# Left operands loaded in place, weight sums on two engines, and a rearranged opening in a Strassen-like gated MLP

## The chip, the cores and the metric

The kernel runs on one core of a Trainium2 chip. The metric is the device time of one execution in microseconds; lower is better. All arithmetic is in 32-bit floats. TensorE (PE) reads them as fp32r, which drops low bits, so each operand is split into a high part and a low part and a product is made of three: high x high, high x low, low x high.

## The reference, cut to what matters

```python
x = A_x                                   # 2048 x 576
g = sigmoid((x * gate_w).sum(-1, keepdims=True))
a = linear_attention(x, wqkv) @ wo        # 32 heads
h = gelu(x @ w_gate) * (x @ w_up)         # 576 -> 4608
b = h @ w_down                            # 4608 -> 576
return g * a + (1 - g) * b
```

## The kernel before, in words

There are three stages. The first, up to about 271 us, makes the attention part and stores g * a to DRAM. It isn't touched.

**Gate and up chains.** `x @ w_gate` and `x @ w_up` are done by Strassen's scheme with seven block products (`PRODUCTS`; `product`, whose matmuls are at L854) instead of eight. One chain is one matrix (GATE or UP), one block n of 256 of the 4608 columns, and one half p of the rows; `CHAINS` lists all 72. A product is 7 matmuls of 128x128 by 128x512. Chain c runs in two frames: in frame c its products 1, 6 and 2, in frame c+1 its products 7, 5, 3 and 4, interleaved with the next chain's by the order `FRAME = 1, 7, 5, 3, 6, 2, 4`. So a frame has seven slots, and `(frame, slot)` is an address. Everything that isn't a product is put at such an address with `put(frame, i, do)`; what stands at an address is issued behind that slot's product, and each engine executes in the order of issue.

A chain takes four PSUM banks from a pool of eight: "a" and "b" at slot 0 (the seed of "b" is a ScalarE copy of "a"), "d" at slot 2 and "c" at slot 4. Of its four result blocks, number 0 comes from "a", 3 and 1 from "d" and "b" after additions on VectorE (DVE, `d_sum` is the ScalarE copy of the fifth product, L967; the additions are L969, L972, L979, L982), 2 from "c". A gate chain runs gelu over them (L929) into SBUF; an up chain multiplies onto that (`up`, L932). The blocks live in `e` (p = 0) and `f` (p = 1).

The weights W[GATE] and W[UP] have seven blocks each: three raw ones and four sums. `w_fetch` (L858) loads the four raw blocks into `wraw` and lets GpSimd (POOL) add the sums into `tsum` (`weight_sums`, L373); for (1, UP) the sums come from DRAM (`ws_d`, L860). `w_split` makes the high part on ScalarE (ACT, L868) and the low part on POOL (L869, L870). For the second half of the rows, X[1] is built in the first frames: blocks A11, A12, A22 by DMA (`X_AT`, L1266), the four sums in six pieces (`S_AT`, `s_make`: ACT L1224, then DVE or POOL L1225; `s_load` L1219), each piece through one of two halves of `f`.

**What down needs.** `h @ w_down` is done with 26 products of blocks of h (`DOWN`, one line each: left operand, weight sum, seed, which accumulators it goes to, which weight sums are made for it). The left operands (sums and differences of h blocks named "a7b6" and the like) are made on DVE during the chains by `extras(c)` (`add` L992, `sub` L995), a table by frame and slot relative to chain c, and stored to DRAM (L1004); `get` loads parts back (L1010). For the last chain (LAST = 71) the entries after a certain address are kept in a list `late` and done during the first down units.

**Down units.** A product is cut in three (c = 0, 1, 2), so there are 78 units, `UNITS[u] = (m, c)`. A unit is 36 matmuls 128x128 by 128x288 (L1340). Unit u's left operand (768 KB) is loaded to one of up to four raw buffers (`h_load`, L1196) and split by `h_make`: high part on ACT (L1203, L1206), low part on DVE (L1204, L1207), into `hb[u % 4]`. Its weight is split by `make`: high on ACT (L1173), low on POOL (L1174). Weight sums (`sums`, L1168) go to DVE if the product's left operand has one part and to POOL if it has two; the tiles `vt` come by `fetch` (L1157). The main loop runs `unit(u, 0)`, then `h_make(u + 3)`, `w_make(u + 3)`, `w_sums(u + 4)`, `later()`, `unit(u, 1)`, `later()`. When a product is complete (c = 2), DVE adds its banks onto the accumulators that read it (L1350); a product with "c" in its line goes on in the same banks, so its matmuls wait for those adds. The three first units' operands and weights are prepared by addresses in the last frames.

Of the kernel before, what the change touches and what calls it, by code (L numbers as in the profile page):

```python
# [11 lines left out]
OP = mybir.AluOpType  # L12
# [102 lines left out]
def tile_gated_mix(ctx, tc, xt, xs, xn, wk, wv, wq, wo, wgu, wdn, cst, out):  # L115
# [805 lines left out]

    def chain(c):
# [3 lines left out]
        d_sum = mid["p1"]  # L926
# [4 lines left out]
        def up(i, src):  # L931
            nc.vector.tensor_tensor(es[i], src, es[i], OP.mult)  # L932
# [31 lines left out]
        def s5():  # L964
            d = bank()
            product(p, 5, w, d, True)
            nc.scalar.activation(d_sum, d, AF.Copy)  # L967
            if m == GATE:
                nc.vector.tensor_tensor(es[3], ps["c"], d_sum, OP.add)  # L969
                gelu(3)  # L970
            else:
                nc.vector.tensor_tensor(d, ps["c"], d_sum, OP.add)  # L972
                up(3, d)
# [38 lines left out]
    def extras(c):  # L1012
# [7 lines left out]

        def do(op, o, a, b, name=None):
            def run():
                op(o, a, b)
                if name:
                    keep_h(g, name, o)
            return run
# [35 lines left out]
        return {(-1, 5): [get("7", r0), get("x", r1), get("y", r2)],  # L1062
                (0, 3): [get("6", e[0])],
                (0, 4): [get("5", e[3])],
                (0, 5): [do(add, e[1], e[1], f[0])],
                (0, 6): [do(add, e[1], e[1], r0, "a7b7")],
                (1, 0): [do(sub, e[0], e[0], f[0], "a6b6"), do(add, r0, r0, f[0], "a7b6")],
                (1, 1): [do(sub, r2, f[0], r2, "ayb6")],
                (1, 2): [do(add, s0, s0, f[3])],
                (1, 3): [do(add, s0, s0, e[3], "a5b5"), get("4", r0), get("9", r2)],  # L1070
                (1, 4): [do(add, e[3], e[3], f[3], "a5b4"), do(add, s1, f[0], f[1], "bx")],
                (1, 5): [do(add, r1, r1, s1, "axbx"), do(add, f[1], f[1], f[3], "bz")],
                (1, 6): [do(sub, r0, r0, f[3], "a4b4"), hold("b8", f[2])],
                (2, 0): [do(sub, e[2], f[2], e[2]), do(add, e[2], e[2], r2, "a9b9")],
                (2, 1): [do(add, s2, s1, f[3], "by"), get("8", r1)],
                (2, 3): [do(add, s1, r2, f[2], "a9b8")],
                (2, 4): [do(sub, r2, s2, r2, "a9by")],
                (2, 5): [do(sub, r1, f[2], r1, "a8b8")]}

# [18 lines left out]
    wraw, tsum = (stage[:, c:c + 1536].rearrange("p (i k c) -> p i k c", i=4, k=3) for c in (0, 1536))  # L1098
    es += [e123[:, i] for i in range(3)]
# [25 lines left out]
    class Weights:  # L1125


        def __init__(self):
            self.tasks, self.last, self.at, self.free = [], {}, {}, list(range(18))
# [30 lines left out]
        def sums(self, j):  # L1160
            m, c = UNITS[j]
            for name, x, op, y in DOWN[m].made:
# [4 lines left out]
                eng = nc.vector if len(DOWN[m].parts) == 1 else nc.gpsimd  # L1167
# [10 lines left out]
    AHEAD = 4  # L1178
# [10 lines left out]
    loads, raw_of = deque(range(len(UNITS))), {}  # L1189
# [8 lines left out]
    def h_make(j):  # L1198
        if j < len(UNITS):
            h, at = hb[j % 4], raw_of.pop(j)  # L1200
            raw = raw_at[at]
# [6 lines left out]
            raw_free.append(at)  # L1208
# [32 lines left out]

    ALL = (0, 3), (3, 7)
# [4 lines left out]
    for c, m, more in ((2, UP, (2, GATE)), (5, GATE, (2, UP))):  # L1247
        split_at(c, 0, m, (0, 2))
        split_at(c, 1, m, (4, 5))
        split_at(c, 3, m, (5, 6), (3, 4))  # L1250
        split_at(c, 4, m, (2, 3))
        split_at(c + 1, 0, m, (6, 7))
        fetch_at(c + 1, 0, *more)
    split_at(7, 0, UP, *ALL)
    fetch_at(7, 5, 3, GATE)
# [30 lines left out]
    for frame, i, do in ((LAST - 4, 6, lambda: w_sums(0, 2)), (LAST - 1, 1, lambda: h_load()), (LAST - 1, 1, lambda: w_make(0)),  # L1286
                         (LAST - 1, 2, lambda: w_sums(1, 2)), (LAST - 1, 4, lambda: h_make(0)),
                         (LAST - 1, 5, lambda: w_make(1)), (LAST, 0, lambda: w_sums(2, 1)), (LAST, 2, lambda: h_make(1)),
                         (LAST, 3, lambda: w_make(2)), (LAST + 1, 0, lambda: raw_free.extend((1, 2))),
                         (LAST + 1, 0, lambda: h_make(2)), (LAST + 1, 3, lambda: w_sums(3, 0))):  # L1290
        put(frame, i, do)
# [62 lines left out]
    def later():  # L1354
        if late:
            for do in late.pop(0):
                do()
            if not late:
                raw_free.append(3)

    weight.fetch(7)
    h_load()
# [85 lines left out]
```

## Time and profile before

| | |
|---|---|
| median of 3 runs | 1537.33 us (1535.36 to 1538.04) |
| profiled execution | 1533.54 us, of which the span of the program's instructions is 1531.8 |
| PE matmul busy | 1460.6 us, 95% of the span |
| VectorE, ScalarE, GpSimd busy | 959.5, 640.4, 784.0 us |
| mean granted PE clock | 0.983 of full speed |
| DMA | 282.32 MB, 184 GB/s in the mean |

Matmuls are pipelined and their ends are modelled, so PE busy isn't PE at its peak. The chains begin at about 271 us, the down units at 1109.5 us. In a row of the timeline stand start, length, engine, line, operation, names (out <- in), shapes and, in brackets, how long the engine sat idle before it and what ended that. Names have their numbers left out, and pieces cut from one tile have the tile's name: `xo` is also the space for the down operands.

### The profile page before, as it was taken

The page shows a single profiled execution, that of the slowest core. Times are in us where ns is not written, and L with a number is a line of the kernel's source. Part 1 is how long each engine was busy: PE and PEld are TensorE (multiplying, and loading weights), DVE is VectorE, ACT ScalarE, POOL GpSimd, SP SyncE. Part 2 cuts the span into 40 slices and gives each one's busy share as a digit, 9 for nine tenths or more (in the row PEclk, how much of TensorE's full clock was granted, in tenths as well). Part 3 has the DMA queues.
Part 4 walks back from the last instruction along what each step waited for, and adds up shares of the span by engine and source line. Part 5 has one row for each costly group of instructions (what it writes and reads, how often), then busy time and mean ns, then how long its engine had stood idle before and what let it go on. Part 6 is the DMA issues. An engine that isn't in the chain of part 4 may idle for free. (4 is left out here: it accounts for less than half of the span.)

```text
span 1531.8 us, 21118 instructions
## 1 busy us (share of the span) xinstructions
PE 1460.6 (95%) x8096; PEld 1296.4 (85%) x8096; DVE 959.5 (63%) x1121; ACT 640.4 (42%) x863; POOL 784.0 (51%) x505
## 2 busy tenths in 40 slices
PE   9999999889999999999999999999689899989989
PEld 9998899778878878787887878788589889989979
DVE  7887896434384654647455374743778568759474
ACT  7555664434333334333333433333334354435342
POOL 2663451545455454455445545541136885685763
PEclk9999999999999999999999999999889999999999
DMA  7664567642453433536344353547989475665651
GB/s 245 173 191 151 181 212 245 213 170 73 152 206 124 166 136 114 175 124 211 128 142 162 107 200 124 190 147 239 314 317 370 146 245 177 224 233 193 215 184 55
DMA packets 122629, 282.32 MB, mean 184 GB/s; under 512 B 11864, under 2 KB 39064, under 8 KB 121248
## 3 DMA queue, kind: packets, MB, share of 16 engines
q1 hardware_dynamic: 119792, 273.71, 52.7%
q10 hardware_dynamic: 2736, 7.28, 1.3%
q8 instruction: 63, 1.03, 0.3%
q14 instruction: 38, 0.31, 0.1%
HBM read 182.40 MB, written 98.50 MB: 183 GB/s over the span
## 5 line engine op out<-in xcount | busy, mean ns | idle before, releaser
L854 PE MATMUL bank<-xo,wg 128*128 128x512 f32 x1764 | 419.8, 391 | 17.8 <-DVE e L969 9.9
L854 PE MATMUL bank<-xo,wu 128*128 128x512 f32 x1715 | 405.7, 390 | 4.6 <-DVE bank L972 2.9
L854 PEld LDWEIGHTS bank<-xo,wg 128*128 128x128 f32 x1764 | 331.1, 188 | 90.5 <-DVE e L969 12.8
L854 PEld LDWEIGHTS bank<-xo,wu 128*128 128x128 f32 x1715 | 323.2, 189 | 72.9 <-DVE bank L972 3.3
L1340 PE MATMUL bank<-xo 128*128 128x288 f32 x2124 | 294.7, 300 | 28.9 <-DVE acc L1350 27.0
L1340 PEld LDWEIGHTS bank<-xo 128*128 128x128 f32 x2124 | 289.6, 192 | 32.4 <-DVE acc L1350 16.8
L373 POOL TENSOR_TENSOR stage<-stage 128x384 f32<-128x384 f32 x132 | 138.6, 1071 | 178.7 <-DMA stage<-wgu 176.1
L939 ACT ACTIVATE bank<-bank 128x512 f32<-128x512 f32 x139 | 80.9, 582 | 242.1 <-PE bank L854 238.5
L1174 POOL TENSOR_TENSOR xo<-vt,xo 128x864 fp32r<-128x864 f32 x42 | 107.7, 2564 | 78.5 <-ACT xo L1173 76.1
L869 POOL TENSOR_TENSOR wg<-stage,wg 128x768 fp32r<-128x768 f32 (+3 forms) x41 | 73.8, 1800 | 136.5 <-ACT wg L868 131.9
L1174 POOL TENSOR_TENSOR xo<-stage,xo 128x864 fp32r<-128x864 f32 x26 | 68.5, 2635 | 103.2 <-ACT xo L1173 90.6
L869 POOL TENSOR_TENSOR wu<-stage,wu 128x768 fp32r<-128x768 f32 (+3 forms) x38 | 75.7, 1993 | 84.1 <-ACT wu L868 82.5
L972 DVE TENSOR_TENSOR bank<-bank,mid 128x512 f32<-128x512 f32 x36 | 25.1, 697 | 142.7 <-ACT mid L967 142.7
L1340 PE MATMUL bank<-xo,wu 128*128 128x288 f32 x684 | 96.1, 299 | 5.2 <-DVE acc L1350 5.2
L1340 PEld LDWEIGHTS bank<-xo,wu 128*128 128x128 f32 x684 | 93.6, 192 | 5.8 <-issue 3.6
L969 DVE TENSOR_TENSOR f<-bank,mid 128x512 f32<-128x512 f32 x18 | 12.4, 691 | 118.5 <-ACT mid L967 114.2
L967 ACT ACTIVATE mid<-bank 128x512 f32<-128x512 f32 x71 | 42.4, 597 | 96.8 <-PE bank L854 88.6
L1173 ACT ACTIVATE xo<-vt 128x864 fp32r<-128x864 f32 x42 | 38.7, 921 | 81.3 <-POOL vt L1168 53.6
L781 PEld LDWEIGHTS pair<-kw,p 128*128 128x128 f32 x448 | 60.8, 189 | 1.0
L781 PE MATMUL pair<-kw,p 128*128 128x288 f32 x448 | 61.4, 295 | 0.0
L531 PE MATMUL bank<-xo,qw 128*128 128x512 f32 (+1 forms) x231 | 55.7, 392 | 0.0
L932 DVE TENSOR_TENSOR f<-bank,f 128x512 f32<-128x512 f32 x72 | 49.6, 688 | 6.7 <-PE bank L854 5.4
(245 smaller groups left out, 2166.8 us busy)
## 6 DMA issues: line engine op xcount, KB each, us to landing
wg<-h_d SPq DMA_DIRECT2D x39, 768.0 KB, 5.1
stage<-wgu SPq DMA_DIRECT2D x34, 768.0 KB, 4.3
h_d<-sx SPq DMA_DIRECT2D x72, 256.0 KB, 3.5
xo<-h_d SPq DMA_DIRECT2D x22, 768.0 KB, 8.6
h_d<-mid SPq DMA_DIRECT2D x63, 256.0 KB, 4.3
h_d<-e SPq DMA_DIRECT2D x63, 256.0 KB, 3.5
e<-h_d SPq DMA_DIRECT2D x17, 768.0 KB, 4.5
vt<-wdn SPq DMA_DIRECT2D x25, 432.0 KB, 5.5
```

The lines of the kernel that those rows point to most:

```text
L373: nc.gpsimd.tensor_tensor(o, a, b, OP.subtract)
L531: nc.tensor.matmul(ps[:wa.shape[1]], wa, xa, start=(k == 0), stop=(k == len(ops) - 1), skip_group_check=g == 4)
L781: nc.tensor.matmul(y[:, i, :288], p[:, 5 * a + g], KW[g][:, wl, i * 288:(i + 1) * 288], start=(n == 0), stop=(n == 13))
L854: nc.tensor.matmul(ps, w_, x_, start=start and i == 0, stop=i == 6, skip_group_check=not start)
L869: nc.gpsimd.tensor_tensor(w[:, i, 3:5], src[:, :, 0:2], f32(w[:, i, 0:2]), OP.subtract)
L932: nc.vector.tensor_tensor(es[i], src, es[i], OP.mult)
L939: nc.scalar.activation(o, src, AF.Copy)
L967: nc.scalar.activation(d_sum, d, AF.Copy)
L972: nc.vector.tensor_tensor(d, ps["c"], d_sum, OP.add)
L1173: nc.scalar.activation(w[:, 0], src, AF.Copy)
L1174: nc.gpsimd.tensor_tensor(w[:, 1], src, f32(w[:, 0]), OP.subtract)
L1340: nc.tensor.matmul(y, h[:, hl, g, t * 128:(t + 1) * 128], w[:, wl, g * 288:(g + 1) * 288], start=first and c == 0 and n == 0, stop=c == NK ...
```

## The change

1. *First left operands in place.* Units 0, 1 and 2 have their left operand loaded straight into the place of its low part, `hb[u][:, 1]` (`h_direct`), at (LAST-2, 1), (LAST-1, 0) and (LAST, 0); `h_make` then splits it there. The raw buffers begin with unit 3. The splits of units 1 and 2 move from (LAST, 2) and (LAST+1, 0) to (LAST, 4) and (LAST+1, 6).
2. *Weight sums.* They go to POOL for c = 1, and for c = 2 if the product's number is odd, else to DVE. They run five units ahead instead of four. The first weight tiles are fetched at (LAST-4, 6); the sums of unit 3 are made at (LAST, 5), those of unit 4 ahead of the loop.
3. *Two up blocks stay in banks.* In the chains (p = 1, UP, n odd and over 1: eight of them) blocks 0 and 3 are multiplied in place in banks "a" and "d", and the additions of `extras` read them there. One of these additions moves from (2, 1) to (1, 6), one from (2, 0) to (2, 1), and two fetches move by a slot.
4. *Early splits.* The three raw blocks of (1, UP) are loaded at (0, 5) into a space of their own (`wmore`) and split from there; the splits of the first two frames, X pieces and blocks stand at other addresses; the sums of (2, GATE) get an address of their own; the splits of UP at frame 7 come in two parts.
5. *Leftovers.* Two more entries of the last chain go to `late`, which is now served once per unit, not twice. `vt` starts with 15 tiles and gets three more when `late` is empty. Accumulator loads move from units 1, 3, 6 to units 5, 10, 18.

```diff
-        d_sum = mid["p1"]
+        d_sum, in_bank = mid["p1"], m == UP and p == 1 and n > 1 and n % 2 == 1
+        made[c] = ps
...
         def up(i, src):
-            nc.vector.tensor_tensor(es[i], src, es[i], OP.mult)
+            o = src if in_bank and i in (0, 3) else es[i]
+            nc.vector.tensor_tensor(o, src, es[i], OP.mult)
...
+        f0, f3 = ("a", "d") if n else (f[0], f[3])
...
-                (0, 5): [do(add, e[1], e[1], f[0])],
+                (0, 5): [do(add, e[1], f0, e[1])],
...
-                (1, 2): [do(add, s0, s0, f[3])],
-                (1, 3): [do(add, s0, s0, e[3], "a5b5"), get("4", r0), get("9", r2)],
-                (1, 4): [do(add, e[3], e[3], f[3], "a5b4"), do(add, s1, f[0], f[1], "bx")],
+                (1, 2): [do(add, s0, f3, s0), get("4", r0)],
+                (1, 3): [do(add, s0, s0, e[3], "a5b5"), get("9", r2)],
+                (1, 4): [do(add, e[3], f3, e[3], "a5b4"), do(add, s1, f0, f[1], "bx")],
...
-                (1, 6): [do(sub, r0, r0, f[3], "a4b4"), hold("b8", f[2])],
-                (2, 0): [do(sub, e[2], f[2], e[2]), do(add, e[2], e[2], r2, "a9b9")],
-                (2, 1): [do(add, s2, s1, f[3], "by"), get("8", r1)],
+                (1, 6): [do(sub, r0, r0, f3, "a4b4"), do(add, s2, f3, s1, "by"), hold("b8", f[2])],
+                (2, 0): [do(sub, e[2], f[2], e[2]), get("8", r1)],
+                (2, 1): [do(add, e[2], e[2], r2, "a9b9")],
...
-                eng = nc.vector if len(DOWN[m].parts) == 1 else nc.gpsimd
+                eng = nc.gpsimd if c == 1 or c == 2 and m % 2 else nc.vector
...
+    DIRECT = 3
+    loads, raw_of = deque(range(DIRECT, len(UNITS))), {}
+
+    def h_direct(j):
+        nc.sync.dma_start(f32(hb[j][:, 1]), h_d[UNITS[j][1]][:, UNITS[j][0]])
...
-    X_AT = {(0, 5): A11, (2, 6): A12, (3, 6): A22}
-    S_AT = [(0, 4), (2, 0), (3, 1), (3, 3), (3, 5), (4, 0)]
+    X_AT = {(0, 5): A11, (3, 4): A12, (4, 0): A22}
+    S_AT = [(0, 4), (1, 2), (2, 1), (2, 5), (3, 1), (3, 3)]
...
-    split_at(0, 5, GATE, (4, 6))
+    put(0, 5, lambda: nc.sync.dma_start(wmore, wgu[1, 1][:, 1:]))
+    split_at(1, 0, GATE, (4, 6))
     split_at(1, 1, GATE, (2, 3), (3, 4), (6, 7))
-    fetch_at(1, 1, 1, UP)
...
+    put(1, 6, lambda: nc.sync.dma_start(tsum, ws_d))
+    put(2, 0, lambda: nc.sync.dma_start(wraw, wgu[2, 0]))
+    put(2, 0, lambda: w_split_raw(0, 2))
+    split_at(2, 4, UP, (4, 5))
+    split_at(2, 6, UP, (5, 6), (3, 4))
+    put(3, 0, lambda: w_split_raw(2, 3))
+    split_at(3, 1, UP, (6, 7))
+    put(3, 2, lambda: weight_sums(wraw, tsum))
...
-            if c < LAST or (frame, i) in ((0, 3), (0, 4), (0, 5), (0, 6), (1, 0), (1, 1)):
+            if c < LAST or (frame, i) in ((0, 3), (0, 4), (0, 5), (0, 6)):
...
+    for frame, i, do in ((LAST - 4, 6, lambda: weight.fetch(3)), (LAST - 2, 1, lambda: h_direct(0)),
+                         (LAST - 1, 0, lambda: h_direct(1)), (LAST - 1, 1, lambda: h_load()),
+                         (LAST - 1, 1, lambda: w_make(0)), (LAST - 1, 4, lambda: h_make(0)),
+                         (LAST - 1, 5, lambda: w_make(1)), (LAST, 0, lambda: h_direct(2)),
+                         (LAST, 4, lambda: h_make(1)), (LAST, 3, lambda: w_make(2)), (LAST, 5, lambda: weight.sums(3)),
+                         (LAST + 1, 0, lambda: (raw_free.extend((1, 2)), h_load())),
+                         (LAST + 1, 6, lambda: h_make(2))):
...
     weight.fetch(7)
-    h_load()
     acc_load(1)
+    w_sums(4)
     for u in range(len(UNITS)):
         unit(u, 0)
         h_make(u + 3)
         w_make(u + 3)
-        w_sums(u + 4)
-        later()
+        w_sums(u + 5)
         unit(u, 1)
         later()
-        if u in (1, 3, 6):
-            acc_load((0, 2, 3)[(1, 3, 6).index(u)])
+        if u in (5, 10, 18):
+            acc_load((0, 2, 3)[(5, 10, 18).index(u)])
```

More of the change, by code (lines that the diff above doesn't have):

```diff
@@ L920, in tile_gated_mix @@
     FRESH = {(1, "b"): 0, (1, "c"): 1, (2, "b"): 2}
+    made = {}
     def chain(c):
@@ L964, in s5 @@
         def s5():
-            d = bank()
+            d = ps["d"] = bank()
             product(p, 5, w, d, True)
@@ L1128, in __init__ @@
         def __init__(self):
-            self.tasks, self.last, self.at, self.free = [], {}, {}, list(range(18))
+            self.tasks, self.last, self.at, self.free = [], {}, {}, list(range(15))
             used = {}
@@ L1199, in h_make @@
         if j < len(UNITS):
-            h, at = hb[j % 4], raw_of.pop(j)
-            raw = raw_at[at]
+            h, at = hb[j % 4], raw_of.pop(j, None)
+            raw = raw_at[at] if j >= DIRECT else f32(h[:, 1])
             if all(minus for minus, _, _ in DOWN[UNITS[j][0]].parts):
```

51 lines of the change are left out of this document (29 added, 22 removed).

## Prediction

> **What bounds the kernel now.** I read the page first, then a table of stretches cut where the kind of work changes, then the waits of TensorE (PE), and last the timeline around each wait.
>
> ```profile
> span 1531.8 us, 21118 instructions
> ```
>
> In the table the columns are the stretch, its length, then busy time of PE, of its weight loads, of VectorE (DVE), ScalarE (ACT) and GpSimd (POOL), the granted clock, and DMA share and rate.
>
> ```profile
> 271.40:330.00 58.60, 50.08 (x206) 40.03 (x205) 25.23 (x32) 22.94 (x37) 31.55 (x32) 0.94 0.60 218
> 330.00:1073.50 743.50, 733.61 (x3228) 605.13 (x3227) 395.18 (x514) 273.92 (x398) 355.63 (x261) 1.00 0.45 153
> 1073.50:1109.50 36.00, 23.03 (x78) 17.20 (x77) 26.15 (x31) 10.60 (x14) 4.35 (x2) 0.80 0.90 315
> 1109.50:1137.00 27.50, 20.25 (x130) 20.01 (x129) 23.33 (x22) 9.04 (x8) 9.48 (x4) 0.82 0.85 307
> 1137.00:1531.80 394.80, 364.69 (x2681) 360.85 (x2680) 271.81 (x196) 169.24 (x154) 262.07 (x92) 0.97 0.61 208
> ```
>
> PE is the bound nearly everywhere: what it loses is idle time (length less its busy time) and the clock below 1. Idle is 8.5 us in the first stretch (opening gate and up chains), 9.9 in the second (steady chains), 13.0 in the third (last frames), 7.3 in the fourth (first down units), 30.1 in the fifth. So the change is priced stretch by stretch, by the waits that it removes and the new ones it makes.
>
> **A, opening chains.**
>
> ```profile
> 282.88 1.88 PE L854 MATMUL bank<-xo,wu 128*128 128x512 f32 x7 [1.68 <-ACT sx L937]
> ...
> 295.40 0.52 ACT L868 ACTIVATE wu<-stage 128x384 fp32r<-128x384 f32 x1 [1.33 <-DMA stage<-ws_d]
> ...
> 297.19 4.80 PE L854 MATMUL bank<-xo,wu 128*128 128x512 f32 x14 [2.91 <-DVE bank L972]
> ...
> 323.26 3.24 PE L854 MATMUL bank<-xo,wg 128*128 128x512 f32 x8 [3.93 <-POOL xo L1225]
> ```
>
> Three waits. The first is on ACT, which copies the seed after a split of two blocks; the split now stands behind it, which frees about 0.7 us. In the second, ACT sat on the landing of the stored sums before it could copy the fifth product; the raw blocks now come early into a space of their own and the sums are split three slots later. In the third, PE waits for the last X piece; it is now made four slots earlier. On POOL it stands behind the splits of five blocks and the weight sums, and by my estimate of that queue it is done about a microsecond before need. After the second and third the clock was half for a while: 0.06 of 58.6 is 3.5 us. In all 8.5 + 3.5 = 12. What I see left is 1.0 us of the first wait, and about 0.7 later, because an X piece now stands ahead of a seed addition on DVE, behind which the copy for the next product queues. SP gains the early load of the three raw blocks and the refetch of the raw weights two frames sooner; both wait for buffers that are read out by then. With a microsecond for shifts in the queues that I can't follow I take **9 us gained** (5 to 11, the low end if the last X piece is late after all). The split of frame 7 in two parts and the fetches one slot later I cost at nothing: their first user is the next chain on that matrix, most of a frame away; without that cover a split part would cost its ACT time, 0.5 at 295.40 for a third of it.
>
> **B, steady chains.**
>
> ```profile
> PE bank L854 <- DVE e L969: 9.9, 7, 2.8
> ```
> ```profile
> 529.05 1.39 DVE L992 TENSOR_TENSOR e<-e,f 128x512 f32<-128x512 f32 x1
> ...
> 529.86 9.68 PE L854 MATMUL bank<-xo,wg 128*128 128x512 f32 x42
> ...
> 530.36 0.68 DVE L992 TENSOR_TENSOR sx<-f 128x512 f32<-128x512 f32 x1
> ...
> 533.48 2.35 DVE L995 TENSOR_TENSOR e<-f,e 128x512 f32<-128x512 f32 x1
> ...
> 537.17 2.89 DVE L992 TENSOR_TENSOR sx<-sx,f 128x512 f32<-128x512 f32 x1
> ...
> 540.71 1.89 PE L854 MATMUL bank<-xo,wg 128*128 128x512 f32 x7 [1.17 <-DVE e L969]
> ```
>
> Seven times, once per eight frames, DVE is so far behind that PE waits: six waits sum to 7.1 and one is 2.8. Additions whose two sources both lie in SBUF (1.39, 2.35, 2.89) are stretched while POOL works; those with a source in a bank are not:
>
> ```profile
> L932 DVE TENSOR_TENSOR f<-bank,f 128x512 f32<-128x512 f32 x72 | 49.6, 688 | 6.7 <-PE bank L854 5.4
> ```
>
> The change makes the 2.89 and the 1.39 bank-sourced: 2.2 + 0.7 us less ahead of L969, more than the 1.17 needed, so those waits go. But the block in bank "a" now lives until its last reader, the addition at 530.36. With eight banks and four taken per chain, "a" comes round again two chains later, and that is the product that starts at 529.86. With 0.7 us saved ahead of it that reader runs from 529.66 to 530.34: PE waits 0.5 us there, each time. Gain 6 x (1.17 - 0.5) + (2.8 - 0.5) = **6 us** (3 to 8).
>
> The Trainium skill (SBUF — State Buffer, Who interferes with whom) says that a VectorE instruction with two SBUF inputs contends with GpSimd reads and one with a single SBUF input does not. These rows agree.
>
> **C, last frames.**
>
> ```profile
> 1068.87 0.69 DVE L995 TENSOR_TENSOR mid<-mid,f 128x512 f32<-128x512 f32 x1 [3.84 <-DMA mid<-ha_d]
> ...
> 1073.53 1.75 PE L854 MATMUL bank<-xo,xo 128*128 128x512 f32 x7
> ...
> 1075.39 0.68 DVE L992 TENSOR_TENSOR sx<-f 128x512 f32<-128x512 f32 x1
> ...
> 1087.70 2.68 PE L854 MATMUL bank<-xo,wg 128*128 128x512 f32 x7 [3.52 <-DVE f L969]
> ...
> 1094.09 7.23 PE L854 MATMUL bank<-xo,xo 128*128 128x512 f32 x21 [3.71 <-ACT bank L939]
> ...
> 1105.03 0.69 DVE L995 TENSOR_TENSOR r<-f,r 128x512 f32<-128x512 f32 x1 [3.27 <-DMA r<-ha_d8y]
> ...
> 1106.39 3.35 PE L854 MATMUL bank<-xo,xo 128*128 128x512 f32 x7 [5.07 <-DVE bank L972]
> ```
>
> Eleven products of 1.6 us (six took 9.68 above) are 17.7 us of work in a stretch of 36. The 3.52 and 3.71 come from ACT and DVE, which stand on left operands that have not landed and, once they have, split them ahead of the chains' own steps. Direct loads start up to a frame earlier, and the second and third split move two to six slots back, behind the steps that PE waits for. The 5.07 comes from an addition (1105.03) that waited for its DMA; it moves into the down units. The first five weight tiles are fetched three frames earlier, where the DMA share is 0.45. Added on SP are the three direct loads (768 KB, 2.5 us each at 315 GB/s); the first stands ahead of the fetch that DVE awaits at 1068.87, and delays it by 0 to 2.3 us; I take 1.5. From there DVE works without a pause to the end of the "a" reader: 1075.39 + 0.68 - 1068.87 = 7.2, so until 1077.6. The product due at 1073.53 now takes over that bank and waits 4.1 us (2.5 to 5), and I put 2 us of half clock behind it. I keep 1 us before the last product. New length 17.7 + 4.1 + 2 + 1 = 24.8: **11 us gained** (3 to 15; the DMA share of 0.90 is why the low end is so low).
>
> **D, first down units.**
>
> ```profile
> 1109.77 1.78 SPq L1157 DMA_DIRECT2D vt<-wdn  x4
> ...
> 1116.64 1.06 DVE L1168 TENSOR_TENSOR vt<-vt,vt 128x864 f32<-128x864 f32 x1 [3.86 <-DMA vt<-wdn]
> ...
> 1132.49 16.29 PE L1340 MATMUL bank<-xo 128*128 128x288 f32 x108 [7.25 <-DVE acc L1350]
> ```
>
> DVE's backlog of leftover additions made the 7.25; at one slot per unit instead of two it goes, and so does the DVE part of the first sums. The accumulator loads that are put off to units 5, 10 and 18 have six units or more until they are read; I cost that at nothing, or one wait of DVE for a landing if the queue is full. But the two sums each of units 4 and 5 move from DVE (1.06) to POOL, where one takes 3.56 and a low part 2.06 (rows under E). Counting from the first unit: loads land after 6.9, I say 8, as two left-operand loads are issued just before; sums of unit 4 until 15.1; low part of unit 3 until 17.2, which PE wants at 14.7; sums of unit 5 until 24.3; low part of unit 4 until 26.4, wanted at 22.0 (a unit is 4.77, and its first three matmuls, 0.4, need no low part). Two waits, 2.5 + 4.4, and 2.5 for the clock: 9.4. Before: 7.25 and half of a low clock beside work, about 10. **1 us gained** (-4 to 5).
>
> **E, the other down units.**
>
> ```profile
> 1172.48 14.48 PE L1340 MATMUL bank<-xo 128*128 128x288 f32 x108
> ```
> ```profile
> 1439.52 3.56 POOL L1168 TENSOR_TENSOR vt<-vt,vt 128x864 f32<-128x864 f32 x1
> ...
> 1443.11 0.93 ACT L1173 ACTIVATE xo<-vt 128x864 fp32r<-128x864 f32 x1 [4.31 <-POOL vt L1168]
> ...
> 1444.12 2.06 POOL L1174 TENSOR_TENSOR xo<-vt,xo 128x864 fp32r<-128x864 f32 x1 [1.04 <-ACT xo L1173]
> 1445.45 2.34 DVE L1204 SCALAR_TENSOR_TENSOR xo<-wg,xo 128x1536 fp32r<-128x1536 f32 x1 [3.17 <-ACT xo L1203]
> 1446.13 3.55 POOL L1168 TENSOR_TENSOR stage<-stage 128x864 f32<-128x864 f32 x1
> ...
> 1472.77 3.38 POOL L1174 TENSOR_TENSOR xo<-stage,xo 128x864 fp32r<-128x864 f32 x1
> ...
> 1476.99 1.75 DVE L1207 TENSOR_TENSOR wu<-wg,wu 128x1536 fp32r<-128x1536 f32 x1
> ...
> 1478.66 2.86 DVE L1168 TENSOR_TENSOR vt<-sx,stage 128x864 f32<-128x864 f32 x1
> ...
> 1482.51 7.62 PE L1340 MATMUL bank<-xo 128*128 128x288 f32 x36 [5.21 <-DVE acc L1350]
> ```
>
> Three units (x108) take 14.48, or 14.32 without the modelled end of the last matmul: 4.77 a unit, 0.1326 a matmul. The 2681 matmuls would need 355.5, so 39 us of 394.8 are lost, about 3 of them after the last matmul, where nothing changes; 36 are open to the change. The clock has 0.03 x 394.8 = 12 of them, 3 to 4 for each of three long waits. Products whose sums all lie on POOL run at 3.56 + 0.93 + 2.06 + 0.1 = 6.6 us per unit against PE's 4.8 and eat the three units of lead; where DVE has all sums it takes 3 x 2.9 + 3 x 2.3 + 2 to 4 for the accumulator adds, 18 to 20 against 14.3. Then the adds, on which the next product in the same banks waits, come late. Now column third 0 goes to DVE, 1 to POOL, and 2 by the product's parity. From the table of products, POOL goes from 21 sums to 29, DVE from 33 to 25. The worst product for POOL has 2 x 3.56 + 3 x 2.56 = 14.8, its neighbours 11.2 or 7.7; for DVE 2 x 2.9 + 3 x 2.3 + 2 = 14.7. And with sums one unit earlier, the low part no longer waits for the copy of a sum just made, and no DVE sum falls between the two halves' adds of a product's last unit. I leave 9 us for products with two reads and for jitter: **27 us gained** (10 to 33).
>
> The 2.56 is the mean of the largest group of low parts, the 2 to 4 are four to eight adds of 0.5:
>
> ```profile
> L1174 POOL TENSOR_TENSOR xo<-vt,xo 128x864 fp32r<-128x864 f32 x42 | 107.7, 2564 | 78.5 <-ACT xo L1173 76.1 <-DMA wg<-h_d 2.0
> ...
> L1350 DVE SCALAR_TENSOR_TENSOR acc<-bank,probe,acc 128x288 f32<-128x288 f32 x48 | 23.2, 506 | 14.6 <-PE bank L1340 14.6
> ```
>
> **Sum.** 9 + 6 + 11 + 1 + 27 = 54 us off the profiled execution's 1533.54 (its span plus 1.7), 1479.5. The median of the runs, 1537.33, is 3.8 above that execution; with it, **1483 us**.
>
> **Rivals.**
>
> R1, contention takes half of E: more POOL and DVE work at once pushes low parts from 2.56 towards the 3.38 of 1472.77 and DVE's sums stay at 2.9. E gives 13: 1497 us. For it: both engines near 14.5 of 14.3 in the worst products; against: their neighbours have room. Chance 0.2.
>
> R2, the last frames are DMA-bound: 0.90 share already, and the same bytes in less time. Fetches for the leftover additions and the first sums come late; C gives 3 and D loses 4: 1496 us. Chance 0.13.
>
> R3, **slower**: POOL and DVE exclude each other. A POOL low part then waits out DVE's 1.75 and costs 3.8; the nine later odd products with sums need 3 x 3.8 + 7.1 = 18.5 against 14.3, each with 3.4 of low clock behind its wait: 68 us, and the seven even ones 5 more. E becomes 36 - 73 = -37 and the kernel 10 us slower, 1547. It decides from a mean low part of about 3.6. Against it: at 1446.13 POOL started inside DVE's 2.34 and still took its 3.55. Chance 0.05. The Trainium skill's section named above calls the shared pair an exclusive lock, the loser fully blocked; by that rule this rival is the forecast, but these two rows do not bear it out.
>
> R4, the banks are not handed round as I count, and the new waits of B and C don't arise: 10 us more, 1473. Chance 0.07.
>
> **Numbers.** My forecast has 0.55. The range 1464 to 1508 takes in R1, R2 and R4 and the bounds of C and E. Runs of this kernel can tell about 0.2%, 3 us. Faster 0.94, same 0.02, slower 0.04.
>
> **What would show it.** In the changed profile: no wait on L969 at the seven places but 0.5 us on an addition reading bank "a" a frame earlier; a wait of 3 to 5 us at the first product of the last chain; PE waiting on POOL L1174 in the fourth and fifth units; 29 POOL sums of 3.6, low parts under 2.8, and few waits on L1350. I am wrong if low parts average above 3.3, if the last frames still take over 32 us, or if the opening shows a wait over 2 us.

## The result and the profile after

The changed kernel takes 1466.78 us (median of four runs, 1465.62 to 1467.03) beside 1537.68 us for the kernel before on the same chip: a ratio of 0.9534, 95% interval 0.9511 to 0.9557. The forecast was 1483, in a range of 1464 to 1508, so the time lies 2.8 us above the range's low end. The profiled execution took 1465.62 us, 67.9 less than the one before, where the prediction had 54.

The table of stretches of the changed kernel, cut at the same matmuls as the prediction's table (opening, steady chains, last frames, first down units, the rest; columns as there):

```profile
core 0 of [0], span 1463.8 us
core 0: us, PE busy (x) PEld busy (x) DVE busy (x) ACT busy (x) POOL busy (x), PEclk, DMA share, GB/s
270.83:319.00 48.17, 47.20 (x206) 37.92 (x205) 23.75 (x32) 22.79 (x37) 32.22 (x32) 1.00 0.71 261
319.00:1052.40 733.40, 731.74 (x3228) 605.59 (x3227) 385.71 (x513) 278.59 (x401) 352.83 (x262) 1.00 0.46 157
1052.40:1076.20 23.80, 18.76 (x78) 14.49 (x77) 20.36 (x28) 9.90 (x12) 2.55 (x2) 0.98 0.96 354
1076.20:1096.30 20.10, 18.36 (x129) 18.09 (x128) 12.67 (x13) 3.79 (x3) 10.70 (x5) 0.94 0.95 358
1096.30:1463.80 367.50, 357.48 (x2682) 356.25 (x2680) 305.12 (x201) 171.03 (x157) 311.76 (x100) 0.99 0.67 231
```

Idle time of TensorE is now 1.0, 1.7, 5.0, 1.7 and 10.0 us by stretch (length less PE's busy time), where it was 8.5, 9.9, 13.0, 7.3 and 30.1. VectorE and GpSimd are busier in the last stretch (305 and 312 us, from 272 and 262 in the longer one before), in part because more of the leftover additions fall there, in part because their instructions take longer beside each other (a low part on GpSimd 3.05 us in the mean, from 2.62). GpSimd also makes 29 weight sums instead of 21, VectorE 25 instead of 33.

The waits of TensorE in these stretches of the changed kernel (us in total, times, longest):

```profile
PE bank L1374 <- DVE acc L1384: 7.6, 2, 5.9
PE bank L854 <- DVE bank L976: 5.0, 2, 3.3
PE bank L854 <- ACT bank L943: 1.7, 2, 1.5
...
PE bank L1374 <- POOL xo L1184: 0.9, 1, 0.9
PE bank L854 <- ACT sx L941: 0.8, 1, 0.8
...
PE bank L854 <- DMA wg<-wp_d: 0.3, 1, 0.3
PE bank L854 <- DVE f L973: 0.2, 1, 0.2
```

The seven waits on the fifth product's addition (L969 before, L973 now) are gone but for one of 0.2 in the last frames, and no wait on an addition that reads bank "a" took their place. The waits on the accumulator adds, the first line, were the largest group in the kernel before:

```profile
PE bank L1340 <- DVE acc L1350: 32.2, 10, 7.2
```

Lines L976, L1374, L1178, L1184 and L1384 are the L972, L1340, L1168, L1174 and L1350 of before.

I timed each matmul against the matmul of the same number in the trace of before. The gain grew by 10.4 us until frame 15 (A), 12.1 from there to frame 70 (B), 10.2 from frame 70 to the first down unit (C), 6.2 in units 0 to 4 (D) and 28.5 from unit 5 on (E), with 0.6 ahead of the opening. Predicted were 9, 6, 11, 1 and 27.

### The profile page after: what moved, and what is told of

It is laid out like the page before. It is cut to its first block, busy times and chain, and to the rows that moved or that the text cites. A ratio compares the mean times of both kernels' runs of the same rounds, so it can differ in the third digit from the quotient of the medians.

```text
span 1463.8 us, 21091 instructions
## 1 busy us (share of the span) xinstructions
PE 1442.5 (99%) x8096; PEld 1285.8 (88%) x8096; DVE 965.4 (66%) x1113; ACT 640.7 (44%) x863; POOL 831.3 (57%) x513
## 5 line engine op out<-in xcount | busy, mean ns | idle before, releaser
L1374 PE MATMUL bank<-xo 128*128 128x288 f32 x2124 | 288.4, 297 | 8.6 <-DVE acc L1384 7.6
L1374 PEld LDWEIGHTS bank<-xo 128*128 128x128 f32 x2124 | 285.2, 190 | 10.0 <-ACT wu L1220 6.1
L373 POOL TENSOR_TENSOR stage<-stage 128x384 f32<-128x384 f32 x132 | 135.4, 1048 | 161.1 <-DMA stage<-wgu 158.4
L1184 POOL TENSOR_TENSOR xo<-vt,xo 128x864 fp32r<-128x864 f32 x38 | 118.2, 3120 | 30.2 <-ACT xo L1183 30.2
L869 POOL TENSOR_TENSOR wu<-stage,wu 128x768 fp32r<-128x768 f32 (+2 forms) x36 | 73.0, 2028 | 90.0 <-ACT wu L868 85.7
L976 DVE TENSOR_TENSOR bank<-bank,mid 128x512 f32<-128x512 f32 x36 | 25.1, 696 | 140.3 <-ACT mid L971 140.3
L1184 POOL TENSOR_TENSOR xo<-stage,xo 128x864 fp32r<-128x864 f32 x28 | 82.9, 2967 | 51.9 <-ACT xo L1183 51.9
L1374 PE MATMUL bank<-xo,wu 128*128 128x288 f32 x684 | 93.6, 295 | 0.0
L973 DVE TENSOR_TENSOR f<-bank,mid 128x512 f32<-128x512 f32 x18 | 12.4, 692 | 121.0 <-ACT mid L971 116.8
L1374 PEld LDWEIGHTS bank<-xo,wu 128*128 128x128 f32 x684 | 91.6, 188 | 0.0
L1221 DVE TENSOR_TENSOR xo<-wg,xo 128x1536 fp32r<-128x1536 f32 x24 | 59.9, 2496 | 12.9 <-ACT xo L1220 12.9
L1220 ACT ACTIVATE xo<-wg 128x1536 fp32r<-128x1536 f32 x24 | 35.7, 1489 | 46.8 <-PE bank L1374 22.3
```

What stands on the lines that cost most here:

```text
L373: nc.gpsimd.tensor_tensor(o, a, b, OP.subtract)
L869: nc.gpsimd.tensor_tensor(w[:, i, 3:5], src[:, :, 0:2], f32(w[:, i, 0:2]), OP.subtract)
L1184: nc.gpsimd.tensor_tensor(w[:, 1], src, f32(w[:, 0]), OP.subtract)
L1220: nc.scalar.activation(h[:, 0], raw, AF.Copy)
L1221: nc.vector.tensor_tensor(h[:, 1], raw, f32(h[:, 0]), OP.subtract)
L1374: nc.tensor.matmul(y, h[:, hl, g, t * 128:(t + 1) * 128], w[:, wl, g * 288:(g + 1) * 288], start=first and c == 0 and n == 0, stop=c == NK ...
```

## The experiments

The theory to test was the prediction's own, with one doubt from the trace: the wait that it expected on bank "a" never came. Three questions follow. Was the count of banks wrong, or the wait hidden? Are the engines of the weight sums the cause of E, or the lead of five units? And what do the last frames and the first units wait for? Each kernel is the changed one with one edit unless it says otherwise; medians are over four or five runs, ratios are against the kernel before on the same chip (the changed kernel: 0.9534).

### Fixed banks

```diff
-    both.banks(8)
+    both.banks(5)
+    two_a = [fixed_bank.tile([128, 512], F32, name=f"bank_a{i}") for i in range(2)]
+    one_d = fixed_bank.tile([128, 512], F32, name="bank_d")
...
-            a = ps["a"] = bank()
+            a = ps["a"] = two_a[c % 2]
...
-            d = ps["d"] = bank()
+            d = ps["d"] = one_d
```

> The changed kernel, but with bank "a" of the chains alternating between two fixed banks and the fifth product's bank fixed, as the kernel before had them by its order of freeing; five banks stay for the rest. Theory of the prediction (B and C): the first product of chain 71 then takes the bank that the addition at 1054.68 to 1055.36 still reads, so it starts at about 1055.4 instead of 1052.42, 3 us late with up to 2 us of half clock behind it; later waits of 1.52 and 3.30 may take back up to 4 of it; the steady groups cost at most 0.1 each, as their reader ends at 517.35 where the frame starts. Together 1 to 5 us over the changed kernel's 1466.8, and a wait of TensorE on VectorE L996 at that product. Rival: the place of the banks makes no difference, because the allocation was never the limit: no such wait, 1466 to 1468.

Measured: 1470.38 us, ratio 0.9553 (0.9537 to 0.9569). The interval overlaps that of the changed kernel, so here the trace decides, not the time. First the changed kernel's timeline at chain 71's first product, then the same place with fixed banks:

```profile
1052.42 1.76 PE L854 MATMUL bank<-xo,xo 128*128 128x512 f32 x7
...
1054.68 0.68 DVE L996 TENSOR_TENSOR sx<-bank,f 128x512 f32<-128x512 f32 x1
```

```profile
1056.65 0.68 DVE L996 TENSOR_TENSOR sx<-bank_a,f 128x512 f32<-128x512 f32 x1
...
1057.39 1.88 PE L854 MATMUL bank_a<-xo,xo 128*128 128x512 f32 x7 [2.83 <-DVE sx L996]
```

In the changed kernel the product runs 2.3 us ahead of the addition that reads chain 69's bank "a", so it can't be in the same bank. The bank numbers in the two programs say why: before, chains 13 and 15 both have "a" in bank 0, and 69 and 71 too. In the changed one they have it in banks 0 and 7, and 7 and 0: the pool hands out the bank that has been free longest in the order of issue, and a bank that is held longer simply drops back in that order. With the old places forced, the predicted wait appears, 2.83 of the predicted 3. In the steady chains one wait of 0.36 is on such an addition, and the seven groups lose 2.3 us in all, more than the 0.1 each I had expected and less than the 0.5 each of the prediction. A wait of 1.20 in the opening is on the fifth product's fixed bank.

### The two up blocks back in SBUF

```diff
-        d_sum, in_bank = mid["p1"], m == UP and p == 1 and n > 1 and n % 2 == 1
+        d_sum, in_bank = mid["p1"], False
...
-        f0, f3 = ("a", "d") if n else (f[0], f[3])
+        f0, f3 = f[0], f[3]
```

> The changed kernel, but the two up blocks of every eighth chain go to SBUF again and the additions read them there; the additions stay where the change moved them. Theory of the prediction (B): the additions with two SBUF sources are stretched to 1.4 to 2.9 again and the seven waits on L973 come back at 1.2 to 1.5 each: 8 to 12 us slower than 1466.8, 1475 to 1479. Rival: moving one addition out of the last frame of the group is what removed the waits; the banks add nothing: 0 to 3 us slower, no or short waits on L973.

Measured: 1478.49 us, ratio 0.9608 (0.9591 to 0.9625). All seven waits are back, as the waits of this run show:

```profile
PE bank L854 <- DVE e L973: 10.2, 7, 2.8
```

The same addition in both traces, for the group around frame 23, first with the blocks in SBUF, then in the changed kernel:

```profile
518.21 1.39 DVE L996 TENSOR_TENSOR e<-f,e 128x512 f32<-128x512 f32 x1
...
522.65 2.34 DVE L996 TENSOR_TENSOR sx<-f,sx 128x512 f32<-128x512 f32 x1
```

```profile
516.06 0.69 DVE L996 TENSOR_TENSOR e<-bank,e 128x512 f32<-128x512 f32 x1
...
519.79 0.68 DVE L996 TENSOR_TENSOR sx<-bank,sx 128x512 f32<-128x512 f32 x1
```

An addition with one source in a bank takes 0.68, one with both in SBUF 1.39 to 2.34 while GpSimd works. Moving additions alone removed no wait: B is the banks' doing.

### The opening alone

The kernel before, with only the edits of point 4 of the change and the new `X_AT` and `S_AT`.

```diff
-    X_AT = {(0, 5): A11, (2, 6): A12, (3, 6): A22}
+    X_AT = {(0, 5): A11, (3, 4): A12, (4, 0): A22}
...
+    put(0, 5, lambda: nc.sync.dma_start(wmore, wgu[1, 1][:, 1:]))
```

> The kernel before with only the change's edits to the opening chains (raw blocks loaded early into a space of their own, stored sums split later, last X piece made four slots earlier). Theory: the 10.4 us that the changed kernel gained until frame 15 are all the opening's and nothing later takes them back, 1527.3 (10 to 11 off 1537.7). Rival: the steady waits on L969 are fixed to when data land, so part is given back: 3 to 8 us off.

Measured: 1526.65 us, ratio 0.9924 (0.9905 to 0.9944); of 1537.68 us that is 11.7 off, 8.6 to 14.6 by the interval. Until frame 5 the trace is 10.6 us ahead of before. In its profiled execution the waits later happened to be longer and left 3.1 of it; the timed runs keep 11, so the opening is worth what the changed kernel shows there.

### First direct load later

```diff
-(LAST - 2, 1, lambda: h_direct(0))
+(LAST - 2, 5, lambda: h_direct(0))
```

> The changed kernel, but the first direct load of a left operand is issued four slots later, behind the two fetches of the last leftover additions. Theory: it was this load that made the fetch land 2.3 us later than before, and with it the wait of 1.66 on the addition onto a bank: that wait goes, 1 to 2 us faster than 1466.8 if the later waits (1.52, 3.30) don't grow. Rival: the DMA queues are full there whatever the order, or the later waits take it back: 1466 to 1468.

Measured: 1468.08 us, ratio 0.9542 (0.9524 to 0.9559). The wait of 1.66 went, and one of 1.81 on L973 came in the same chain (0.21 before); at the first slot of frame 72 both kernels are equally far (28.3 us ahead of before). The rival holds: the load did delay the fetch, but undoing that brought nothing that the runs can tell.

### First weight sums later

```diff
-(LAST, 5, lambda: weight.sums(3))
+(LAST + 1, 3, lambda: weight.sums(3))
```

> The changed kernel with the first weight sums moved from the last chain's frame into the frame behind it, three slots from its start, where the kernel before had them. Theory: these two sums on VectorE (2.20 us) stand ahead of the leftover addition and the addition onto a bank that TensorE awaits for 3.30 us, and 3.41 us of half clock follow: the wait shrinks by 2.2 and the clock stays, 2 to 4 us faster than 1466.8. Rival: the sums are then late for the low part of unit 3, and the time is lost again there: 1466 to 1468.

Measured: 1468.11 us, ratio 0.9549 (0.9533 to 0.9565). The wait shrank from 3.30 to 1.35 and unit 0 began 3.2 us sooner, but this run's TensorE then shows

```profile
1076.12 8.61 PE L1374 MATMUL bank<-xo 128*128 128x288 f32 x63 [1.70 <-DVE f L936]
...
1093.71 1.57 PE L1374 MATMUL bank<-xo 128*128 128x288 f32 x5 [1.94 <-POOL xo L1184]
```

and by unit 4 it is 2.7 us behind the changed kernel. The rival holds.

### The engines and the lead of the weight sums

Four kernels: all sums on VectorE; the old engines with the new lead; the new engines with the old lead; both old.

```diff
-                eng = nc.gpsimd if c == 1 or c == 2 and m % 2 else nc.vector
+                eng = nc.vector
```

> The changed kernel with all weight sums on VectorE. Theory of the prediction (E): the split of the sums over two engines is what gained, and a VectorE with all sums of a product needs 18 to 20 us against 14.3 and its accumulator adds come late: waits on L1384 come back, 10 to 30 us slower than 1466.8. Rival, the exclusive pair: VectorE and GpSimd shut each other out while both use SBUF operands, so only the sum of their work counts: a pair of low parts takes 1.75 + 2.05 = 3.8, a sum 1.06 on VectorE and 2.05 on GpSimd; all on VectorE makes 78 x 3.8 + 54 x 1.06 = 354 us against TensorE's 372, 29 less than now: no slower, 1462 to 1468.

```diff
-                eng = nc.gpsimd if c == 1 or c == 2 and m % 2 else nc.vector
+                eng = nc.vector if len(DOWN[m].parts) == 1 else nc.gpsimd
```

> The changed kernel with the sums on the engines that the kernel before chose (VectorE for products of one part, GpSimd for products of two), still five units ahead. Theory of the prediction (E): the split by column third carries most of the 28.5 us gained in the down units, so 15 to 27 us slower than 1466.8. Rival: calling the sums one unit earlier carries it: 0 to 6 us slower. The exclusive pair says that the old choice has 21 sums on GpSimd instead of 29, 374 us of pair work instead of 382: not slower by work, only by its order.

```diff
-    AHEAD = 3
+    AHEAD = 4
...
-    w_sums(4)
...
-        w_sums(u + 5)
+        w_sums(u + 4)
```

> The changed kernel with the sums called four units ahead, as before the change, on the new engines. Theory of the prediction (E): the engine split is the main thing, four ahead costs 3 to 8 us by sums that fall between the adds of a product's last unit. Rival: the lookahead is the main thing: 15 to 27 us slower than 1466.8.

Both of the last two diffs together:

> The changed kernel with both the engines of the sums and the four units of lead as before the change; chains, direct loads and accumulator loads stay changed. If the two parts add up (10.6 for the engines, 15.2 for the lead) the time is 1492.6. Theory of the prediction (E and D, with nearly all of 28 us in the sums): 1492 to 1497. Rival: the two parts replace each other, as either takes sums out of VectorE's way between the accumulator adds, so the loss is more than their sum: 1497 or above; or the accumulator loads carry a part, then below 1490.

Measured, with the gain against the kernel before that the trace makes from the first matmul of unit 12 to the end:

| engines | lead | median us | ratio (interval) | gain from unit 12 on |
|---|---|---|---|---|
| by column third (changed) | 5 | 1466.78 | 0.9534 (0.9511 to 0.9557) | 34.4 |
| all on VectorE | 5 | 1478.76 | 0.9620 (0.9601 to 0.9640) | 26.2 |
| as before | 5 | 1477.38 | 0.9610 (0.9591 to 0.9629) | 30.3 |
| by column third | 4 | 1482.01 | 0.9638 (0.9622 to 0.9655) | 19.1 |
| as before | 4 | 1502.27 | 0.9773 (0.9758 to 0.9788) | -1.2 |

With both undone nothing is left of the gain from unit 12 on, so there the sums are all of it. Against that kernel the lead alone brings 31.5 (30.3 + 1.2), the engines alone 20.3 (19.1 + 1.2), both 35.6: either does most of the work, and they replace each other; undoing both costs 10 us more than the sum of undoing each. The prediction had put the gain on the engines. Ahead of unit 12 the old engines lose 6.9 as well, with a wait of 9.0 at unit 3. With both undone, the waits on the accumulator adds are back nearly as they were:

```profile
PE bank L1374 <- DVE acc L1384: 28.7, 10, 6.6
```

How the lead does it is seen in ScalarE's copies and GpSimd's instructions where all sums of a product are on GpSimd. With the old engines and the old lead:

```profile
1317.68 0.93 ACT L1183 ACTIVATE xo<-sx 128x864 fp32r<-128x864 f32 x1 [4.32 <-POOL sx L1178]
1318.51 1.47 ACT L1220 ACTIVATE xo<-wg 128x1536 fp32r<-128x1536 f32 x1
1318.69 2.06 POOL L1184 TENSOR_TENSOR xo<-sx,xo 128x864 fp32r<-128x864 f32 x1 [1.04 <-ACT xo L1183]
...
1320.02 2.35 DVE L1221 TENSOR_TENSOR xo<-wg,xo 128x1536 fp32r<-128x1536 f32 x1 [3.43 <-ACT xo L1220]
1320.71 3.56 POOL L1178 TENSOR_TENSOR stage<-f,stage 128x864 f32<-128x864 f32 x1
...
1324.31 0.93 ACT L1183 ACTIVATE xo<-stage 128x864 fp32r<-128x864 f32 x1 [4.32 <-POOL stage L1178]
```

With the old engines and the new lead:

```profile
1306.05 0.91 ACT L1183 ACTIVATE xo<-sx 128x864 fp32r<-128x864 f32 x1
...
1307.40 2.06 POOL L1178 TENSOR_TENSOR stage<-f,stage 128x864 f32<-128x864 f32 x1
...
1307.87 3.20 DVE L1221 TENSOR_TENSOR xo<-xo 128x1536 fp32r<-128x1536 f32 x1
1309.41 3.59 POOL L1184 TENSOR_TENSOR xo<-sx,xo 128x864 fp32r<-128x864 f32 x1
...
1310.82 0.91 ACT L1183 ACTIVATE xo<-stage 128x864 fp32r<-128x864 f32 x1
```

In the first, ScalarE waits 4.32 for a sum that GpSimd has only just been given; the next operand's copy (L1220) stands behind it, VectorE's split (L1221) behind that. The loop closes in 6.63 us per unit (1317.68 to 1324.31) and VectorE's adds come late. In the second, sum and copy belong to different units: the copy starts at once, and the period is TensorE's 4.77 (1306.05 to 1310.82). From unit 12 on ScalarE waits 117 us for weight sums in the first and 22 in the second. On the new engines it waits 131 us with the old lead and 14 with the new: the lead removes these waits on either engines. What the new engines do with the old lead is another thing: ScalarE waits as long, but TensorE's waits on the adds from unit 12 on fall from 24.1 us (longest 6.6) to 12.8 (longest 2.5). That fits a loop that no longer holds all three units of a product, which no run tried by itself.

All sums on VectorE costs nothing between units 4 and 60 (15.2 us of gain grow there, 14.6 in the changed kernel). It loses 8 at unit 3 and 6 in units 60 to 65, the latter with a wait of 2.60 on the adds and half clock behind it. At unit 3 the reason is a sum that waits for its weights and holds up everything behind it on VectorE:

```profile
1086.17 1.06 DVE L1178 TENSOR_TENSOR vt<-vt,vt 128x864 f32<-128x864 f32 x1 [5.67 <-DMA vt<-wdn]
...
1099.92 0.58 PE L1374 MATMUL bank<-xo 128*128 128x288 f32 x1 [7.80 <-DVE acc L1384]
```

So the rival by the sum of work (354 against 382 us, no slower) held from unit 4 to 60 and fell for the whole kernel: what it lost at unit 3 came of the order in a queue, not of the total. In the changed kernel the same wait for weights falls on GpSimd, which had nothing urgent there.

### Attempts at a faster version

Unit 12 of the changed kernel waits longest, and half clock follows:

```profile
1143.66 1.78 PE L1374 MATMUL bank<-xo 128*128 128x288 f32 x6 [5.89 <-DVE acc L1384]
```

```diff
-        if u in (5, 10, 18):
-            acc_load((0, 2, 3)[(5, 10, 18).index(u)])
+        if u in (3, 13, 20):
+            acc_load((0, 2, 3)[(3, 13, 20).index(u)])
```

> The changed kernel with the accumulator loads at units 3, 13 and 20 instead of 5, 10 and 18. Theory: from 1116 to 1160 the DMA queues are full (share 0.9 to 1.07, about 400 GB/s), and the accumulator loads of units 5 and 10 are the 2.3 MB too many: the left operand issued at 1122.73 landed only at 1130.4, so VectorE had its split and a sum of 2.85 still ahead of the accumulator adds when unit 12 wanted their banks. At unit 3 the queues are at 0.4 to 0.7, and unit 13 lies behind the wait. Then the 5.89 and its half clock shrink by 3 to 6 us: 1461 to 1464. Rival: the adds are late by VectorE's own work (leftover additions at 2.5 each beside GpSimd), so the wait stays within 1 us and the time is 1466 to 1468.

Measured: 1469.55 us, ratio 0.9558 (0.9542 to 0.9574); the wait is 4.18, unit 12 begins at 1143.13. The wait shrank by 1.7, less than the theory asked and more than the rival, and the time did not fall. Then, in addition:

```diff
-(LAST, 5, lambda: weight.sums(3))
-(LAST + 1, 6, lambda: h_make(2))
+(LAST + 1, 6, lambda: (h_make(2), weight.sums(3)))
```

> As the run before, and with the first weight sums put behind the last chain's last products and the third left operand's split, instead of ahead of the additions of the last chain. Theory: the 3.30 wait at the second last product shrinks to 1.2 and the half clock of 3.41 behind it goes, 3 to 4 us before the down units start; with the moved accumulator loads 1457 to 1461. Rival: the first down units wait for weights that land at 1085 to 1087 whatever comes before, as the run with the first sums three slots into the frame showed (3.2 us ahead at unit 0, 2.7 behind at unit 4): all of it is given back by unit 5, and the time is that of the run before.

Measured: 1468.11 us, ratio 0.9554 (0.9538 to 0.9569). Unit 0 began 4.35 us sooner, unit 4 1.6, unit 12 0.5. Then, in addition:

```diff
-        later()
+        if u % 3 != 2:
+            later()
```

> As the run with the accumulator loads and the first sums moved, and with the twelve steps of leftover additions spread: none in the third unit of each product, so eight of them are done by unit 11 instead of all twelve. In that run unit 12 began at 1143.1 though unit 0 had begun 4.35 us earlier than in the changed kernel, and VectorE had no gap above 0.25 us from 1098.2 to 1142.5. Theory: VectorE is the bound of units 4 to 11, because its additions from SBUF take 2.5 beside GpSimd instead of 0.68; four additions less ahead of the accumulator adds are 7 to 10 us less there, the 6.80 wait shrinks to at most 1 and its half clock goes; with what comes back at units 15 to 18 it is 4 to 8 us faster than 1466.8: 1459 to 1463. Rival: the queues are the bound (share about 1.0 from 1116 to 1160), the left operand of unit 11 lands when it does, and the wait stays at 4 or more: 1465 to 1468.

Measured: 1467.63 us, ratio 0.9541 (0.9522 to 0.9560). The wait at unit 12 is 6.74: my theory fell, and none of the three beats the changed kernel. Unit 12 starts between 1142.8 and 1145.1 in seven of the twelve kernels that have all or most of the change (the changed one, these three, and those with the later direct load, the later first sums and both parts of the sums undone), though their unit 0 starts from 1071.9 to 1077.6. (In the other five it starts later, from 1145.7 to 1156.5.) One stretch, from unit 4 to the adds of unit 11, in the run before the spreading and in the run with it:

```profile
1098.20:1142.50 44.30, 38.04 (x285) 37.81 (x285) 44.30 (x27) 20.49 (x22) 29.68 (x13) 0.99 0.91 314
```

```profile
1099.00:1143.90 44.90, 38.86 (x291) 38.63 (x289) 43.75 (x24) 23.09 (x24) 33.49 (x14) 0.96 0.81 292
```

VectorE is busy through all of it with 27 instructions and nearly so with 24. Of its 2.5 us for a leftover addition only 0.68 is its own time, as the rows in the last section show; the rest is read as the wait for GpSimd's low part, which has to be done anyway. Worked out from the shortest durations (0.5, 0.68, 1.04 and 1.74 on VectorE, 2.06 on GpSimd), the changed kernel has 27.5 us of VectorE's and 20.6 of GpSimd's work in the 45.2 us from unit 4 to unit 12; the sum, 48.1, is a little more than the time, and VectorE's adds from a bank can lie beside GpSimd's work. That the pair of engines is the bound there fits all runs but is only argued; keeping GpSimd's sums out of that stretch alone wasn't tried.

## Why the prediction was right and where it was wrong

In sum the prediction fell 14 us short of the profiled 67.9: 6 of them in B, 5 in D, and about 1.5 each in A and E. The range was wide enough to hold that; the sizes of C and E owe part of their agreement to luck, as said below.

**A** was right: 9 predicted, 10.4 measured, 11.7 with its interval of 8.6 to 14.6 by the opening alone.

**B** had the right mechanism and a wrong cost beside it: 6 against 12.1. The failing step is "with eight banks and four taken per chain, 'a' comes round again two chains later": true of the kernel before, whose order of freeing it took over, and not of the changed one. Without the 0.5 us wait 6 x 1.17 + 2.8 = 9.8 would have been the sum; the other 2.3 are 0.3 per group, as each frame with a wait was 1.5 longer, not 1.17. The price of the wait was too high as well: with the old places forced, the seven groups lose 2.3 us, not 7 x 0.5.

**C** was right in size (11 and 10.2) by two errors that cancel. The same step put 4.1 us of wait and 2 of half clock at chain 71's first product, which weren't there; with fixed banks the wait is there, 2.83, and no half clock. In their place came waits of 1.66, 0.21, 1.52 and 3.30, and 3.4 us of half clock that fall mostly in unit 0. The 3.30 comes of the sums of unit 3, to which the prediction gave no place on VectorE ahead of the last chain's additions; taking them away gains nothing in the end.

**D** was undersized, 1 against 6.2. The step is the 3.56 for a sum on GpSimd:

```profile
1085.44 2.31 POOL L1178 TENSOR_TENSOR vt<-vt,vt 128x864 f32<-128x864 f32 x1 [18.12 <-DMA vt<-wdn]
...
1087.84 2.05 POOL L1178 TENSOR_TENSOR stage<-vt,stage 128x864 f32<-128x864 f32 x1
```

The four in units 0 to 3 took 2.46 in the mean and 2.05 at least, as VectorE worked little there, and the weights landed 9.2 us after unit 0 began, not 8. The predicted waits of 2.5 and 4.4 on GpSimd were one of 0.89, with one of 1.74 on VectorE's adds ahead of it.

**E** was right in size, 27 and 28.5, with the cause in the wrong order: the lead, named last and without a price, is worth 31.5 from unit 12 on by itself, the engines 20.3, both 35.6. The size is luck in part: 28.5 is 34.4 gained from unit 12 on, less 5.9 lost ahead of it, where the kernel before has no wait in units 5 to 11. Of the 36 us that the prediction called open 7.5 are left, and they are the one wait of 5.89 at unit 12 with the half clock behind it, not the "products with two reads and jitter" for which it left 9. What holds up unit 12 stays open, as said above. The prediction's period of 6.6 us per unit was right, but it is the loop from sum to copy to sum that takes so long, and one unit more of lead opens it on the old engines too. The Trainium skill (Perfetto Trace Analysis, Optimizing Scalar/DVE Operations) warns that moving work between VectorE and GpSimd might not help, as they share a port; here it helped, by 20.3 us of the median with the old lead and by 10.6 with the new (from unit 12 on alone 20.3 and 4.1).

**The rivals.** R4 (no new waits on banks) is what happened; with 1473 it was nearer than the forecast. R1's premise came and its price did not: low parts grew from 2.62 us in the mean to 3.05, over the 2.8 that the prediction named as its sign, but E gave 28.5, not 13, and TensorE waits for a low part once, 0.89. R2 did not come: the DMA share rose to 0.96 in the last frames, and they took only 23.8 us. R3 (GpSimd and VectorE exclude each other) was put aside on a misread row. The 3.55 of 1446.13 in the trace of before is not a sum that ignored VectorE: alone it takes 2.06, as the run with the old engines shows at 1307.40. The exclusion was already in every row, so it could not be a further loss; low parts now average 3.05 us, below R3's 3.6. The Trainium skill (SBUF — State Buffer, Who interferes with whom) calls the port pair that the two share an exclusive lock. These runs agree, with 2.06 against 3.56 to 3.59.

## What to carry to other kernels

Ask which instruction an in-order queue is given just ahead of one that others await; a lead of one step more on its producer can be worth as much as moving the work to another engine, and the two must be tried alone and together. Before a duration is used as a price, look whether the neighbour's instruction lies inside it: the time of a blocked instruction need not be saved by removing it. Where buffers come from a pool, count them in the changed order of issue, not in the old one.

## What the runs showed of the hardware that was not expected

The price of meeting is nearly the whole instruction of the other engine. These two rows of the changed kernel, an addition beside a low part of GpSimd and one without, show it:

```profile
1109.94 2.55 DVE L996 TENSOR_TENSOR sx<-f 128x512 f32<-128x512 f32 x1
...
1120.69 0.68 DVE L999 TENSOR_TENSOR mid<-mid,f 128x512 f32<-128x512 f32 x1
```

A sum of 864 columns takes VectorE 1.05 alone and 2.91 beside GpSimd, an addition of 512 columns 0.68 and 2.55; GpSimd's sum takes 2.06 alone and 3.57 beside VectorE's split of 1.75. The additions with one source in a bank, in the rows above, took 0.68 or 0.69.

The granted clock fell to half after some waits and not others. In the changed kernel it fell behind the wait of 3.30 and within that of 5.89 (in a row of the windows the clock is the third value from the end):

```profile
1075.40:1078.80 3.40, 3.40 (x14) 3.21 (x13) 3.02 (x5) 0.43 (x1) 0.00 (x0) 0.50 0.95 330
...
1143.66:1147.00 3.34, 3.34 (x14) 3.34 (x15) 3.34 (x5) 0.94 (x2) 3.08 (x1) 0.50 1.03 408
```

It lasted 3.4 us the first time and 6.8, from 1140.25 on, the second. Behind the wait of 2.83 with fixed banks it stayed at 1.00; behind one of 2.79 with the blocks in SBUF it was 0.55 in the mean of 3.8 us. The clock records of the 14 traces show what makes the difference. In each trace the half-clock stretches begin on one grid of 3.413 us. From 250 us on, all 50 full-clock steps of that grid that were followed by half clock had 1.79 us or more in which TensorE was idle, by the modelled ends of its matmuls; of the 4869 that were followed by full clock, none had more than 1.73, but for one with 1.85. The wait of 2.83 lies across two steps, 1.49 and 1.34 us, that of 2.79 within one. So what counted was idle time of about half a grid step, not the length of one wait. The Trainium skill (TensorE: Matmul & The Clock Gate, What's actually happening) describes an activity window of about 3.4 us that runs freely; the grid agrees with it.
